# Pooled attention and gated MLP on one core: stages cut into one-engine parts with a written place for each, and other groupings in two transposes

## The chip, the cores and the metric

The kernel runs on one core of a Trainium2 chip. The metric is device time in microseconds (us) of one execution, less is better. The kernel before takes 604.04 us (median of three runs, 603.68 to 604.25).

## The reference, cut to what matters

Eight batches of 576 rows. Keys and values are averaged over groups of eight rows (72 pooled rows), eight heads of 64 columns attend to them, and the result (576 x 512) goes through a gated MLP whose spatial gate mixes the 576 rows.

```python
k_p = k.reshape(B, H, Sp, pool, D).mean(axis=3)          # Sp = 72, pool = 8
v_p = v.reshape(B, H, Sp, pool, D).mean(axis=3)
scores = scale * np.matmul(q, k_p.transpose(0, 1, 3, 2))
attn = np.exp(scores - max); attn = attn / (sum + 1e-09)
x = np.matmul(attn, v_p)                                 # heads side by side: (8, 576, 512)
h = np.maximum(x @ w_in, 0.0); u, v = h[..., :512], h[..., 512:]
v_n = (v - mean) / np.sqrt(var + 1e-06)
v_s = np.einsum('ts,bsd->btd', w_spatial, v_n) + b_spatial[None, :, None]
out = (u * v_s) @ w_out
```

`w_in` and `w_out` come in as 64-bit floats; all else is 32-bit.

## The kernel before

The 576 rows of a batch are five row tiles: four of 128 and a last one of 64 (tile 4). They are worked on in two halves, tiles 0 and 1 (256 rows) and tiles 2 to 4 (320 rows). The large products run in three passes over operands that are each split into a high and a low part (`_h`, `_l`).

A batch is a list of named stages, each a Python generator that yields between its parts:

- **K** loads the keys and sums each group of eight (on DVE), **KT** transposes the sums on TensorE into PSUM and copies them into the block-diagonal `kp_bd`. The 8 x 72 key rows stand one after the other in blocks of 128, so there are four full blocks and one of 64; the sum is written twice side by side (`kp`, 128 x 128 a block), so that a transpose yields it in both partition halves.
- **V**, **W**: the same sums for the values, then their split and masks (`vm_h`, `vm_l`, `vr`).
- **Q**c loads row tile c of the queries and transposes it; **S**c computes its scores and its softmax; **T**c transposes the probabilities P. A head pair has 144 score columns; the first 128 are transposed at once (`pm`), and the last 16 of all four pairs, the "rest of P" (`pr`, 64 columns), by themselves, in two transposes of 32 columns, into `rr`.
- S has two forms. In the plain one DVE subtracts the maximum, ACT takes one exponential over 576 columns and DVE sums. In the other (marked `~`) ACT takes eight exponentials of 72 columns with the maximum as bias and the sum as by-product.
- **A**hg multiplies P and the values for half h and head pair g into `xT`.
- **v**c, **u**hd: the two halves of x @ w_in (v by row tile with its normalisation, u transposed by half and block of 128 columns); **s**hd: the spatial product and the gate; **o**c: the product with w_out and the store. **o4** stores the last 64 rows of two batches at once.
- **wv**, **wu**, **wo**, **ws**, **wb**: loads and splits of the weights, once, spread over the first stretch of the program. A part of `w_in` can take its low part from three matmuls against identities (marked `^`) or from GpSimd (POOL).

Three strings (`FIRST`, `SECOND` for batch 0, `STEP` for all others, the last too) name the stages in an order. A name begins a stage or advances it by one part; `step()` after each v, u, s, o stage advances every stage that is under way by one part; and `needs()` lists what has to stand before a stage begins, so that a name may begin several others. One part often holds instructions of two or three engines. The recording keeps this order on TensorE (PE), DVE, ACT and POOL. The transfers, all on SyncE's queue (SP), are put in order by the framework. Each engine runs its own instructions strictly in its order and waits on semaphores for the others; PSUM has three buffers for the large products, three for transposes and A (`ps_t`), and one of two banks that KT and S share (`ps_s`).

Of the kernel before, what the change touches and what calls it, by code (L numbers as in the profile page):

```python
# [15 lines left out]
ORDERED = {getattr(mybir.EngineType, n) for n in ("PE", "DVE", "Activation", "Pool")}  # L16


# [9 lines left out]
FIRST = (  # L28
    "KT Q0 wv0~^ KT wv1^ Q0 wv0 wv1 S0~ wv0 Q1 wv1 wv0 S1~ S0 V T0 wv1 Q2 wv0 S1 wv2~^ S1 wv2 V wv2 "
    "wv1 wv2 wv2 W "  # L30
)
SECOND = (
# [6 lines left out]
)  # L39
STEP = (  # L40
    "Q1 . u00 u02 -T4 Q0 v1 -A13 -A10 -A12 S0 u01 -A11 v0 v4 S1 v2 Q4 Q2 v3 u03 u13 W T0 S2 u10 u12 "
    "u11 s00 s03 T1 s11 Q3 s01 +K s12 A00 s10 s02 A03 s13 S3 A02 . A01 . o0 S4 o2 T2 o1 +KT +V T3 o4 "
    "o3 "
# [8 lines left out]
def pooled_attention_gmlp(ctx: ExitStack, tc: tile.TileContext, q, k, v, w_in, w_sp, b_sp, w_out, out):  # L52
# [19 lines left out]
    RR = 2 * KR  # L72
    QK = 1.0 / (POOL * float(D) ** 0.5)
# [55 lines left out]
    def split(hi, lo, src):  # L129
        nc.scalar.activation(hi, src, AF.Copy)  # L130
        nc.vector.tensor_tensor(lo, src, f32(hi), op=ALU.subtract)  # L131

    def load_f64(hi, lo, src, alt, st=None):
# [10 lines left out]
        if len(src.shape) == 2:  # L144
            nc.sync.dma_start(out=st, in_=src.bitcast(U32).rearrange("p (n w) -> p n w", w=2))
        else:
            nc.sync.dma_start(out=st.rearrange("p (c n) w -> p c (n w)", c=NK), in_=src.bitcast(U32))
        low, high = st[:, :, 0], st[:, :, 1]
# [7 lines left out]
        nc.scalar.activation(x, high.bitcast(F32), AF.Abs, scale=2.0 ** -112)  # L156
        yield
# [4 lines left out]
        if "~" in alt:  # L162
            nc.vector.scalar_tensor_tensor(z, low, 2.0 ** -52, y, op0=ALU.mult, op1=ALU.mult)
        else:
            scaled = low.bitcast(F32)
            nc.scalar.activation(scaled, low, AF.Copy, scale=2.0 ** -52)
            nc.gpsimd.tensor_tensor(z, scaled, y, op=ALU.mult)
# [10 lines left out]
        else:  # L178
            nc.gpsimd.tensor_tensor(as_w(x), as_w(x), f32(hi), op=ALU.subtract)
            nc.gpsimd.tensor_tensor(lo, as_w(x), as_w(y), op=ALU.add)  # L180
# [28 lines left out]
    def load_w_sp(i):  # L209
# [3 lines left out]
        nc.sync.dma_start(out=st[:m], in_=w_sp[ts, :])  # L213
        a = ps_big()
# [6 lines left out]
        split(wT_h[:, :NC, ts], wT_l[:, :NC, ts], av)  # L221
        for r in range(2):
            nc.scalar.activation(wT_h[r * TL:(r + 1) * TL, NC, ts], t, AF.Copy)
        nc.vector.tensor_tensor(wT_l[:TL, NC, ts], t, f32(wT_h[:TL, NC, ts]), op=ALU.subtract)
# [27 lines left out]
    def att_keys(t, b, alt=""):  # L252

        rows = k[b].rearrange("h (s j) d -> (h s) (j d)", j=POOL)
        kp = pl.tile([P, NC + 1, 2, D], F32, name="kp", tag="kp")
        acc = ps_pool() if "^" in alt else None
        for r in range(2):
            st = pl.tile([P, 2, POOL * D], F32, name="st", tag="kv", bufs=3)
            nc.sync.dma_start(out=st, in_=rows[2 * r * P:2 * (r + 1) * P].rearrange("(n p) f -> p n f", p=P))
            n2 = slice(2 * r, 2 * r + 2)  # L260
            if acc is None:
                pool_sum(st, kp[:, n2])
            else:
                pool_pe(st, acc[:, n2, :])
            yield
        st = load_rest(rows[NC * P:])
        if acc is None:
            pool_sum(st, kp[:TL, NC:], nc.gpsimd if alt else nc.vector)
        else:
            pool_pe(st, acc[:TL, NC:, :])  # L270
            yield
            nc.scalar.copy(kp[:, :NC], acc[:, :NC, :].unsqueeze(2).broadcast_to([P, NC, 2, D]))
            nc.scalar.copy(kp[:TL, NC:], acc[:TL, NC:, :].unsqueeze(2).broadcast_to([TL, 1, 2, D]))
        t["k"] = kp

    def att_keys_t(kp, alt=""):

        kt = ps_s.tile([P, 2 * 512], F32, name="s_ps", tag="s")
        for n in range(NC + 1):
            m = P if n < NC else TL  # L280
            nc.tensor.transpose(out=kt[:, n * P:n * P + m], in_=kp[:m, n, :, :], identity=ident[:m, :m])
        yield
        keys = kt[:, :H * SP].rearrange("p (g e s) -> p g e s", g=NG, e=2)
        for e in range(2):
            es = slice(e * D, (e + 1) * D)
            copy = nc.vector.tensor_copy if alt else nc.scalar.copy
            copy(kp_bd[es, :, e * SP:(e + 1) * SP], keys[es, :, e, :])

    def att_values(t, b, alt=""):
# [6 lines left out]

        for r in range(2):
            g2 = slice(2 * r, 2 * r + 2)
            st = pl.tile([P, 2, POOL * D], F32, name="st", tag="kv", bufs=3)
            nc.sync.dma_start(out=st, in_=rows[g2, :P].rearrange("g p f -> p g f"))  # L300
            if acc is None:
                pool_sum(st, vp[:, g2, :], eng)
            else:
                pool_pe(st, acc[:, g2, :])
            yield
        st = load_rest(rows[:, P:])
        if acc is None:
            pool_sum(st, vq, eng)
        else:
            pool_pe(st, acc[:2 * RR, NG:, :])  # L310
            yield
            if "~" in alt:
                nc.scalar.copy(vp, acc[:, :NG, :])
                nc.scalar.copy(vq, acc[:2 * RR, NG:, :])
            else:
                vp, vq = acc[:, :NG, :], acc[:2 * RR, NG:, :]
# [7 lines left out]
    def att_values_split(vp, vr_s):  # L324
        for e in range(2):
            nc.scalar.activation(vm_h[:, :, e, :], vp, AF.Copy, scale=half_of[:, e:e + 1])
        yield
        for e in range(2):
            nc.vector.scalar_tensor_tensor(vm_l[:, :, e, :], vp, half_of[:, e:e + 1], f32(vm_h[:, :, e, :]),
                                           op0=ALU.mult, op1=ALU.subtract)  # L330
        nc.scalar.activation(vr[0:RR, :, 1, :], vr_s, AF.Copy)
        nc.scalar.activation(vr[2 * RR:, :, 1, :], vr_s, AF.Copy)
        nc.vector.tensor_tensor(vr[RR:2 * RR, :, 1, :], vr_s, f32(vr[0:RR, :, 1, :]), op=ALU.subtract)

    def att_q(t, b, c, alt=""):
# [3 lines left out]
        nc.sync.dma_start(out=qt[:m], in_=q[b, :, c * P:c * P + m, :].rearrange("h p d -> p h d"))  # L339
        qp = ps_tr()  # L340
# [8 lines left out]
    def att_softmax(t, c, alt=""):  # L349
# [12 lines left out]
        nc.vector.tensor_reduce(mx[:m], sv, axis=AX.X, op=ALU.max)  # L362
        e = pl.tile([P, H, SP], F32, name="e", tag="e", bufs=2)
# [9 lines left out]
        else:  # L373
# [3 lines left out]
            for h in range(H):  # L377
# [20 lines left out]
    def att_pt(t, c):  # L398
# [15 lines left out]
        trv = tr[:RR, :2 * m].rearrange("p (r t) -> p r t", r=2)  # L414
        for r in range(2):
            nc.tensor.transpose(out=trv[:, r, :], in_=pr[:m, 2 * r:2 * r + 2, :], identity=ident[:m, :m])
        yield
        split(mh[:, :, cs], ml[:, :, cs], tpv)
        for i in range(2):
            nc.scalar.activation(rr[i * RR:(i + 1) * RR, :, cs], trv, AF.Copy)  # L420
        nc.vector.tensor_tensor(rr[2 * RR:, :, cs], trv, f32(rr[:RR, :, cs]), op=ALU.subtract)
# [276 lines left out]
```

## Time and profile before

| | |
|---|---|
| median of three runs | 604.04 us |
| the profiled execution, its own time | 605.5 us |
| its span, first to last instruction | 603.7 us |
| mean granted TensorE clock | 0.992 |
| read from HBM, written | 36.08 MB, 9.44 MB |

The profile gives each engine's busy time. A matmul's record is longer than its share of the array's time, since the next one starts before it ends; what a matmul costs in a row of others is read from start to start. 32-bit matmuls that are no transposes stand as two records each. Line numbers are those of the kernel before, unless a row of the changed kernel is shown.

### The profile page before, as it was taken

How to read it: one execution, taken by the hardware profiler on the slowest of the kernel's cores; microseconds unless marked ns; L12 is line 12 of the kernel's file. 1: busy time of each engine (PE TensorE's matmuls, PEld its weight loads, DVE VectorE, ACT ScalarE, POOL GpSimd, SP SyncE). 2: the span in 40 equal slices, each digit the busy share in tenths (PEclk: the TensorE clock that was granted, in tenths of full speed). 3: DMA queues.
4: the chain of work that ended last, by engine and by line, in shares of the span. 5: the costliest groups of instructions: out<-in, count | busy, mean ns of one | idle time of the engine just before them, and what ended most of it. 6: DMA issues, size and time to landing. Idle time of an engine off the chain costs nothing.

```text
span 603.7 us, 9827 instructions
## 1 busy us (share of the span) xinstructions
PE 576.5 (95%) x3605; PEld 513.7 (85%) x3605; DVE 407.4 (67%) x854; ACT 296.8 (49%) x758; POOL 219.3 (36%) x280
## 2 busy tenths in 40 slices
PE   3776999999999999999999999999999999999997
PEld 3455989888997989888998889988998889988995
DVE  6799898968767486657866487766965488344520
ACT  3896576464634464254534355344533445343421
POOL 2237447913532064312442045321632135421440
PEclk9997999999999999999999999999999999999999
DMA  9933343271023210250121410242110300010002
GB/s 297 295 95 97 107 116 106 79 222 41 1 88 120 81 36 11 96 166 3 34 90 70 132 36 0 88 134 52 35 45 36 88 1 1 1 53 19 0 2 87
DMA packets 56688, 46.15 MB, mean 76 GB/s; under 512 B 39104, under 2 KB 41152, under 8 KB 56640
## 3 DMA queue, kind: packets, MB, share of 16 engines
q1 hardware_dynamic: 56640, 45.52, 25.4%
q8 instruction: 28, 0.46, 0.3%
q14 instruction: 20, 0.16, 0.1%
HBM read 36.08 MB, written 9.44 MB: 75 GB/s over the span
## 4 chain that ended last, share of the span: by engine, by line
PE 79%; ACT 12%; DVE 6%; issue 1%; DMA 1%; SPq 0%; POOL 0%; ACTq 0%; DVEq 0%
PE mm L557 17%; PE mm L536 16%; PE mm L477 15%; PE mm L517 9%; PE s_ps L355 5%; PE tp L343 3%; PE mm L492 2%; PE tp L412 2%; ACT e L379 2%; ACT ru L520 1%; PE mm L538 1%; PE mm L537 1%; PE tp L431 1%; PE tp L428 1%; PE tp L429 1%
## 5 line engine op out<-in xcount | busy, mean ns | idle before, releaser
L517 PE MATMUL mm<-xT,win_h 128*128 128x320 f32 (+1 forms) x512 | 105.2, 299 | 0.0
L387 POOL TENSOR_TENSOR pm<-e,rs 128x576 f32<-128x576 f32 (+1 forms) x40 | 49.5, 1238 | 117.2 <-DVE rs L384 52.6
L477 PE MATMUL mm<-win_h,xT 128*128 128x512 f32 x256 | 83.5, 407 | 0.0
L517 PEld LDWEIGHTS mm<-xT,win_h 128*128 128x128 f32 x512 | 82.6, 189 | 0.7
L557 PE MATMUL mm<-wout_h,gT 128*128 128x512 f32 x256 | 82.3, 402 | 0.0
L463 POOL TENSOR_TENSOR rstd<-rstd,neg_half 128x1 f32<-128x1 f32 (+1 forms) x40 | 23.5, 588 | 158.1 <-DVE rstd L462 158.1
L536 PE MATMUL mm<-wT_h,vn_h 128*128 128x320 f32 (+1 forms) x256 | 77.7, 303 | 0.8
L517 PE MATMUL mm<-xT,win_l 128*128 128x256 f32 (+1 forms) x256 | 75.7, 296 | 0.0
L536 PE MATMUL mm<-wT_h,vn_l 128*128 128x320 f32 (+1 forms) x256 | 75.5, 295 | 0.0
L536 PE MATMUL mm<-wT_l,vn_h 128*128 128x320 f32 (+1 forms) x256 | 75.4, 294 | 0.0
L548 POOL TENSOR_TENSOR gT<-g,gT 128x256 fp32r<-128x256 f32 x64 | 48.7, 766 | 61.3 <-ACT gT L547 61.3
L547 ACT ACTIVATE gT<-g 128x256 fp32r<-128x256 f32 x64 | 26.6, 417 | 79.3 <-DVE g L541 79.3
L131 DVE TENSOR_TENSOR pt_l<-tp,pt_h 128x512 fp32r<-128x512 f32 (+1 forms) x40 | 25.4, 635 | 49.0 <-ACT pt_h L130 48.7
L557 PEld LDWEIGHTS mm<-wout_h,gT 128*128 128x128 f32 x256 | 46.5, 189 | 11.2 <-issue 1.2
L477 PEld LDWEIGHTS mm<-win_h,xT 128*128 128x128 f32 x256 | 47.0, 191 | 9.4
L541 DVE TENSOR_TENSOR g<-mm,ru 128x320 f32<-128x320 f32 (+1 forms) x64 | 28.3, 448 | 38.5 <-PE mm L538 30.9
L561 ACT COPY ob<-mm 128x512 f32<-128x512 f32 x36 | 21.1, 587 | 64.4 <-PE mm L557 44.5
L355 PE MATMUL s_ps<-kp_bd,qT 128*128 128x144 f32 (+1 forms) x320 | 48.5, 296 | 4.3 <-ACT qT L346 2.2
L477 PE MATMUL mm<-win_l,xT 128*128 128x512 f32 x128 | 51.4, 401 | 0.0
L355 PEld LDWEIGHTS s_ps<-kp_bd,qT 128*128 128x128 f32 (+1 forms) x320 | 43.3, 186 | 9.4 <-ACT e L379 2.7
L557 PE MATMUL mm<-wout_l,gT 128*128 128x512 f32 x128 | 50.7, 396 | 0.0
L536 PEld LDWEIGHTS mm<-wT_h,vn_h 128*128 128x128 f32 x256 | 48.2, 188 | 2.2 <-ACT ru L520 2.0
(136 smaller groups left out, 1353.4 us busy)
## 6 DMA issues: line engine op xcount, KB each, us to landing
st<-in_k SPq DMA_DIRECT2D x16, 512.0 KB, 3.5
qt<-in_q SPq DMA_DIRECT2D x32, 256.0 KB, 2.9
st<-in_v SPq DMA_DIRECT2D x16, 512.0 KB, 3.6
out<-ob SPq DMA_DIRECT2D x32, 256.0 KB, 2.1
stw<-in_moe_w_in SPq DMA_DIRECT2D x8, 512.0 KB, 7.0
st<-in_moe_w_out SPq DMA_DIRECT2D x4, 512.0 KB, 3.4
st<-in_moe_w_spatial SPq DMA_DIRECT2D x4, 288.0 KB, 4.0
st_r<-in_k SPq DMA_DIRECT2D x8, 128.0 KB, 4.5
```

The lines of the kernel that those rows point to most:

```text
L131: nc.vector.tensor_tensor(lo, src, f32(hi), op=ALU.subtract)
L355: nc.tensor.matmul(s_ps[:m, g // 2, (g % 2) * 2 * SP:(g % 2 + 1) * 2 * SP], lhsT=qT[:, g, :m], rhs=kp_bd[:, g, :], start=True, stop=True,)
L387: nc.gpsimd.tensor_tensor(pm[:m], em, rs[:m].unsqueeze(2).broadcast_to([m, H, SP]), op=ALU.mult)
L463: nc.gpsimd.tensor_tensor(rstd[:m], rstd[:m], neg_half[:m], op=ALU.pow)
L477: nc.tensor.matmul(a, lhsT=xT[:, i, o + c * P:o + (c + 1) * P], rhs=w[:, i, DH:], start=(i == 0 and j == 0), stop=(i == NK - 1 and j == 2))
L517: nc.tensor.matmul(a, lhsT=w[:, i, d * P:(d + 1) * P], rhs=xT[:, i, o + ts.start:o + ts.stop], start=(i == 0 and j == 0), stop=(i == NK - ...
L536: nc.tensor.matmul(a, lhsT=x[:, c, ds], rhs=y[:, c, ts], start=(c == 0 and j == 0), stop=False)
L541: nc.vector.tensor_tensor(g, a, t["ru"][:, d, ts], op=ALU.mult)
L547: nc.scalar.activation(dst[:, d, 0, at:at + m], g[:, o:o + m], AF.Copy)
L548: nc.gpsimd.tensor_tensor(dst[:, d, 1, at:at + m], g[:, o:o + m], f32(dst[:, d, 0, at:at + m]), op=ALU.subtract)
L557: nc.tensor.matmul(a, lhsT=src[:, i, x, at:at + m], rhs=w[:, i, :], start=(i == 0 and j == 0), stop=(i == ND - 1 and j == 2))
L561: nc.scalar.copy(ob[:m], a)
```

## The change

It does five things.

1. Every stage is cut at each change of engine (more `yield`s), so that a part holds one engine's instructions. `run()` does nothing but advance the named stage by one part; `needs()`, `step()` and `begin()` are gone, and the strings name every part. SP is among the engines whose order is kept, so loads and stores have their place too. `SECOND` is gone: `FIRST` covers batch 0's attention and the weights up to batch 0's end, `STEP` is used for batches 1 to 6 and `LAST` for batch 7.
2. KT: two heads' first 64 pooled rows stand in one block (`kp`, four head pairs in two blocks of 128 x 128), the last eight rows of all eight heads in another (`kr`, 64 x 128). Three transposes take the place of five, in a `ps_t` buffer instead of `ps_s`. K loads in four transfers and a rest instead of two and a rest; the sums of `kp` are written once and not twice, and four copies instead of two fill `kp_bd`.
3. The rest of P: POOL writes `pr` twice side by side (two instructions), one transpose takes the place of two, and its rows come out twice, so that ACT copies 64 partitions at once for each pair of head pairs. DVE's subtraction is two instructions.
4. The forms chosen differ: the eight-exponential softmax is used for 18 of 40 tiles instead of 7; the value sums run on POOL for seven of eight batches (on DVE before), the rest of the keys on POOL for six of eight (one before); seven low parts of weights come from matmuls against identities instead of five.
5. What of the weights is loaded when: a part of `w_in` is loaded ahead of the keys.

```diff
-ORDERED = {getattr(mybir.EngineType, n) for n in ("PE", "DVE", "Activation", "Pool")}
+ORDERED = {getattr(mybir.EngineType, n) for n in ("PE", "DVE", "Activation", "Pool", "SP")}
 FIRST = (
-    "KT Q0 wv0~^ KT wv1^ Q0 wv0 wv1 S0~ wv0 Q1 wv1 wv0 S1~ S0 V T0 wv1 Q2 wv0 S1 wv2~^ S1 wv2 V wv2 "
...
+    "wv1~^ wv1 wv1 -K wv1 -K wv3~^ -K -Q0 -V -K -K wv1 -K -Q0 wv3 -Q0 wv3 wv2^ -KT wv1 -KT -Q1 -V -V -KT -S0~ "
...
 STEP = (
-    "Q1 . u00 u02 -T4 Q0 v1 -A13 -A10 -A12 S0 u01 -A11 v0 v4 S1 v2 Q4 Q2 v3 u03 u13 W T0 S2 u10 u12 "
...
+    "-s12 -A00 -s00 -A00 -S4 -A00 -s00 -s10 Q1 -s02 +K~ -T2 -s10 -s13 -s02 -s11 -s02 KT v1 -s03 -S4 -s03 KT "
...
 def att_keys_t(kp, kr, alt=""):
-        kt = ps_s.tile([P, 2 * 512], F32, name="s_ps", tag="s")
-        for n in range(NC + 1):
-            m = P if n < NC else TL
-            nc.tensor.transpose(out=kt[:, n * P:n * P + m], in_=kp[:m, n, :, :], identity=ident[:m, :m])
+        kt = ps_tr()
+        for r in range(2):
+            nc.tensor.transpose(out=kt[:, r * P:(r + 1) * P], in_=kp[:, r, :, :], identity=ident)
+        nc.tensor.transpose(out=kt[:, 2 * P:2 * P + 2 * RR], in_=kr[:, 0, :, :], identity=ident[:2 * RR, :2 * RR])
...
 def att_softmax(t, c, alt=""):
-        pr = pl.tile([P, NG, KR], F32, name="pr", tag="pr", bufs=2)
-        nc.gpsimd.tensor_tensor(pr[:m], em[:, 1::2, SP - KR:], rs[:m, 1::2].unsqueeze(2).broadcast_to([m, NG, KR]),
-                                op=ALU.mult)
+        pr = pl.tile([P, 2, 2, RR], F32, name="pr", tag="pr", bufs=2)
+        for i in range(2):
+            sh = [m, 2, 2, KR]
+            nc.gpsimd.tensor_tensor(
...
 def att_pt(t, c):
-        for r in range(2):
-            nc.tensor.transpose(out=trv[:, r, :], in_=pr[:m, 2 * r:2 * r + 2, :], identity=ident[:m, :m])
+        nc.tensor.transpose(out=tr[:, :m], in_=pr[:m], identity=ident[:m, :m])
...
     def run(b, order):
         for name in order.split():
...
-            again = [part for k, part in going if k == key]
-            if again:
-                advance(key, again[0])
-            else:
-                begin(key, **({"alt": name} if name[-1] in "~^" else {}))
-            if name[0] in ".vuso" and not again:
-                step()
+            make = (wl if key[0] < 0 else stages[key[0]] if key[0] < B else {}).get(key[1])
+            if make and key not in parts:
+                parts[key] = make(**({"alt": name} if name[-1] in "~^" else {}))
+            next(parts.get(key, iter(())), None)
```

Three places show how the order moves. First, the head of SP's queue: the transfers with which the program starts. Before:

```order
L259 DMA st<-in_k 128x2x512 x2
L249 DMA st_r<-in_k 64x512
L339 DMA qt<-in_q 128x8x64
L145 DMA stw<-in_moe_w_in 128x1024 x2
L339 DMA qt<-in_q 128x8x64
L300 DMA st<-in_v 128x2x512
```

And in the changed kernel:

```order
L165 DMA stw<-in_moe_w_in 128x1024
L289 DMA st<-in_k 128x1x512 x4
L165 DMA stw<-in_moe_w_in 128x1024
L276 DMA st_r<-in_k 64x1x512
L377 DMA qt<-in_q 128x8x64
L335 DMA st<-in_v 128x2x512
```

One part of `w_in` now stands ahead of all keys, and a second ahead of the rest of the keys and the first queries; batch 0's keys come in four transfers.

Second, PE in the middle of the program, at a KT and a T (`kp` the pooled keys, `pm` the probabilities, `pr` their rest). Before, the KT and the T that follows it between two o stages:

```order
L557 MATMUL mm<-wout_l,gT 128x512
L281 MATMUL s_ps<-ident,kp 128x128 x4
L281 MATMUL s_ps<-ident,kp 128x64
L412 MATMUL tp<-ident,pm 128x128 x4
L416 MATMUL tp<-ident,pr 32x128 x2
L557 MATMUL mm<-wout_h,gt 128x512 x2
```

In the changed kernel KT stands behind tile 4's scores and ahead of an A; this is the piece from there:

```order
L394 MATMUL s_ps<-kp_bd,qT 64x144 x4
L312 MATMUL tp<-ident,kp 128x128 x2
L313 MATMUL tp<-ident,kr 128x64
L477 MATMUL tp<-pt_h,vm_h 128x256
L478 MATMUL tp<-pt_h,vm_l 128x256
```

and a T of the same batch, 14 rows of an s stage later:

```order
L589 MATMUL mm<-wT_l,vb 128x320
L459 MATMUL tp<-ident,pm 128x128 x4
L461 MATMUL tp<-ident,pr 128x128
L587 MATMUL mm<-wT_h,vn_h 128x320
L587 MATMUL mm<-wT_h,vn_l 128x320
```

KT is three transposes instead of five, T five instead of six, and both stand among other stages than before.

Third, POOL in the middle of the program, up to the probabilities that T0 transposes (`rstd` a v stage's reciprocal deviation, `vn_l` its low part, `gT` and `gt` a gate's low part, `st`, `st_r` the loaded values, `vp`, `vq` their sums). Before:

```order
L387 TENSOR_TENSOR pm<-e,rs 64x576
L389 TENSOR_TENSOR pr<-e,rs 64x64
L463 TENSOR_TENSOR rstd<-rstd,neg_half 128x1 x2
L486 TENSOR_TENSOR vn_l<-vv,vn_h 128x512
L387 TENSOR_TENSOR pm<-e,rs 128x576
L389 TENSOR_TENSOR pr<-e,rs 128x64
```

In the changed kernel, the second half of the value sums onward:

```order
L257 TENSOR_TENSOR st<-st 128x2x256
L257 TENSOR_TENSOR st<-st 128x2x128
L262 TENSOR_TENSOR vp<-st 128x128
L513 TENSOR_TENSOR rstd<-rstd,neg_half 128x1
L257 TENSOR_TENSOR st_r<-st_r 64x256
L257 TENSOR_TENSOR st_r<-st_r 64x128
L262 TENSOR_TENSOR vq<-st_r 64x64
L513 TENSOR_TENSOR rstd<-rstd,neg_half 128x1
L601 TENSOR_TENSOR gT<-g,gT 128x256
L601 TENSOR_TENSOR gt<-g,gt 128x64
L513 TENSOR_TENSOR rstd<-rstd,neg_half 128x1
L428 TENSOR_TENSOR pm<-e,rs 128x576
```

The value sums, which were DVE's, now stand in POOL's queue ahead of the first probabilities of the next batch, and a gate's low part between them. On PE there stand, between the v stage whose `rstd` is the last one here (v2) and T0: v4, v3 and Q3. On DVE the row sum of S0 stands directly behind v2's statistics.

More of the change, by code (lines that the diff above doesn't have):

```diff
@@ L286, in att_keys_t @@
             copy = nc.vector.tensor_copy if alt else nc.scalar.copy
-            copy(kp_bd[es, :, e * SP:(e + 1) * SP], keys[es, :, e, :])
+            copy(kp_bd[es, :, e * SP:e * SP + KM], main[es])
+            copy(kp_bd[es, :, e * SP + KM:(e + 1) * SP], rest[es, :, e, :])
+            if e == 0:
+                yield
     def att_values(t, b, alt=""):
@@ L295, in att_values @@
         acc = ps_pool() if "^" in alt else None
+        sts, g2 = [], [slice(2 * r, 2 * r + 2) for r in range(2)]
         for r in range(2):
[L298 to L302, printed above, removed]
-            else:
-                pool_pe(st, acc[:, g2, :])
+            sts.append(pl.tile([P, 2, POOL * D], F32, name="st", tag="kv", bufs=3))
+            nc.sync.dma_start(out=sts[r], in_=rows[g2[r], :P].rearrange("g p f -> p g f"))
             yield
         st = load_rest(rows[:, P:])
+        yield
+        for r in range(2):
+            if acc is None:
+                pool_sum(sts[r], vp[:, g2[r], :], eng)
+            else:
+                pool_pe(sts[r], acc[:, g2[r], :])
+            yield
         if acc is None:
@@ L327, in att_values_split @@
         yield
+        for r in range(2):
+            nc.scalar.activation(vr[2 * r * RR:(2 * r + 1) * RR, :, 1, :], vr_s, AF.Copy)
+        yield
         for e in range(2):
@@ L561, in moe_o @@
         nc.scalar.copy(ob[:m], a)
+        yield
         if c < NC:
@@ L630, in advance @@
-    def advance(key, part):
-        if next(part, True):
-            going.remove((key, part))
-            done.add(key)
-    def step():
-        for key, part in list(going):
-            advance(key, part)
-    def begin(key, **alt):
-        make = (wl if key[0] < 0 else stages[key[0]] if key[0] < B else {}).get(key[1])
-        if key in begun or not make:
-            return
-        whole, first = ([], []) if key[0] < 0 else needs(*key)
-        for other in whole:
-            begin(other)
-            while other not in done:
-                advance(other, next(part for k, part in going if k == other))
-        for other in first:
-            begin(other)
-        begun.add(key)
-        part = make(**alt)
-        next(part)
-        going.append((key, part))
+    parts = {}
@@ L676 @@
+    run(B - 1, LAST)
 _INS = ["q", "k", "v", "moe_w_in", "moe_w_spatial", "moe_b_spatial", "moe_w_out"]
```

138 lines of the change are left out of this document (63 added, 75 removed), and 35 rows, old and new, of tables (FIRST, LAST, SECOND, STEP).

## The prediction

> **What bounds the kernel now.** I read the page's busy times and slices first. The rows are the engines' busy time and count, and PE's busy tenths in 40 slices.
>
> ```profile
> PE 576.5 (95%) x3605; PEld 513.7 (85%) x3605; DVE 407.4 (67%) x854; ACT 296.8 (49%) x758; POOL 219.3 (36%) x280
> PE   3776999999999999999999999999999999999997
> ```
>
> TensorE is the bound from the fifth slice to the last; the four first slices are not full. Busy times by stretch put numbers on that (columns: stretch, length, then PE, PEld, DVE, ACT, POOL busy with counts, granted clock, DMA share, GB/s).
>
> ```profile
> 0.00:49.40 49.40, 28.26 (x131) 19.61 (x132) 37.61 (x90) 36.66 (x120) 15.92 (x24) 0.96 0.73 218
> 54.30:60.00 5.70, 5.70 (x24) 4.64 (x23) 5.43 (x11) 2.30 (x7) 3.24 (x4) 0.70 0.44 121
> 60.00:599.00 539.00, 537.91 (x3432) 485.98 (x3431) 359.58 (x750) 253.68 (x624) 195.67 (x249) 1.00 0.21 63
> ```
>
> From 60 us on PE idles for 539.00 - 537.91 = 1.1 us in all. So two things can make this kernel faster: an earlier start of the dense part, and less work on PE in it. A better order of the other engines has almost nothing left to win there, and something to lose. The start is read in the timeline:
>
> ```profile
> 4.01 1.15 DVE L230 TENSOR_TENSOR st<-st 128x512 f32<-128x512 f32 x2 [3.16 <-DMA st<-in_k]
> 9.25 0.66 ACT L156 ACTIVATE x<-stw 128x512 f32<-128x512 f32 x1 [7.24 <-DMA stw<-in_moe_w_in]
> 49.11 1.11 PE L412 MATMUL tp<-ident,pm 128*128 128x128 f32 x4 [5.10 <-POOL pm L387]
> 49.18 0.20 DVE L384 RECIPROCAL rs<-sm 64x8 f32<-64x8 f32 x1
> 49.30 2.21 DVE L230 TENSOR_TENSOR st<-st 128x512 f32<-128x512 f32 x2
> 52.84 0.68 DVE L131 TENSOR_TENSOR pt_l<-tp,pt_h 128x512 fp32r<-128x512 f32 x1
> 53.67 0.43 PE L412 MATMUL tp<-ident,pm 64*128 64x64 f32 x4 [1.31 <-DVE pt_l L131]
> 54.31 0.72 PE L477 MATMUL mm<-win_h,xT 128*128 128x512 f32 x2
> ```
>
> The first v stage (L477), the marker of the dense part, starts at 54.31 us, right behind T4. DVE is the engine that sets it: 37.61 us of work up to S4's reciprocal (49.38 us), with 49.38 - 4.01 - 37.6 = 7.8 us of waits since its first key sum. Then 4.9 us pass until the first v, with batch 1's key sum (49.30, to 52.9) ahead of the `pt_l` that T4 waited for.
>
> **The change, part by part.** *Start.* Counted in the order, DVE has nearly the same work ahead of S4's reciprocal: seven weight parts, five maxima, both pooled sums, four `xT`; one `z`, one plain softmax more, one T's `pt_l` and `rr` and one `wT_l` fewer, narrower `kp`. By the rows of before that is 38 us, within 0.5 us of the old count. The weight part that is now first on SP should land where the first keys did, at 4.0 us, instead of 9.25; behind ACT's 0.66 us DVE starts at 4.7. Without waits S4's reciprocal ends at 4.7 + 38 = 42.7 us, with all 7.8 us of them at 50.5. Behind it two `pt_l` and an `rr` (2 x 0.68 + 0.5) stand before T4, and no key sum any more: 2.9 us to the first v with T4's own 0.6 and the hops, or 4.9 as before. So the first v starts between 45.5 and 55.4 us. I take half the waits, since DVE gets work of two kinds (weights, keys) from the first microsecond on, and S1's eight exponentials (2.45 us on ACT) become one: 42.7 + 3.9 + 2.9 = 49.5 us. **Term: -4.8 us**, ends -8.8 and +1.1.
>
> *Transposes.* Rows of PE's timeline around a KT and a T:
>
> ```profile
> 328.47 0.80 PE L281 MATMUL s_ps<-ident,kp 128*128 128x128 f32 x5
> 329.20 0.66 PE L412 MATMUL tp<-ident,pm 128*128 128x128 f32 x4
> ...
> 302.58 0.60 PE L412 MATMUL tp<-ident,pm 128*128 128x128 f32 x4
> 303.01 0.38 PE L416 MATMUL tp<-ident,pr 128*32 128x128 f32 x2
> 303.15 0.39 PE L536 MATMUL mm<-wT_h,vn_h 128*128 128x320 f32 x1
> 303.38 0.31 PE L536 MATMUL mm<-wT_h,vn_l 128*128 128x320 f32 x1
> 303.52 0.31 PE L536 MATMUL mm<-wT_l,vn_h 128*128 128x320 f32 x1
> ```
>
> Start to start four transposes take 0.43 us, 0.109 each. The two of `pr` take 0.14, but the matmul behind them keeps the next waiting 0.23 instead of 0.14: the last transpose's share is paid there. So one `pr` transpose less is worth 0.109 us, or 0.03 if that delay stays as it is. KT loses two of its four full transposes (0.22 us of 0.73); the one of 64 rows stays. In batches 1 to 7: 7 x 0.22 + 28 x 0.109 + 7 x 0.06 (tile 4, half the width) = **-5.0 us**; the other end is -2.6. The first batch's fall into the start. More PSUM copies (four into `kp_bd`, two DVE subtractions a T) lie beside PE's work; ACT and DVE have the room (49% and 67% busy).
>
> In the Trainium skill, "TensorE: Matmul & The Clock Gate", Part 4, a transpose of 128 x 128 costs about 275 ns in a kernel. The trace agrees only with that as one record's length; the spacing is 0.109 us, and here the trace is used. By the page the 49 transposes would be worth 13.5 us as an estimate, and the forecast 588 us; the spacing leaves that no chance of its own.
>
> *Weights.* Two more low parts come from three matmuls against identities, later than the first v. One such set, start to start:
>
> ```profile
> 20.65 1.02 PE L173 MATMUL mm<-x,ident 128*128 128x512 f32 x2
> 21.98 0.60 PE L343 MATMUL tp<-ident,qt 128*128 128x128 f32 x4
> ```
>
> 1.33 us each: **+2.7 us**, or nothing if both fall into idle time.
>
> *Moves to ACT and POOL.* Eleven more tiles take the softmax of eight exponentials, and seven batches sum their values on POOL:
>
> ```profile
> 15.71 2.45 ACT e L379 x16
> 57.86 1.77 POOL L230 TENSOR_TENSOR st_r<-st_r 64x256 f32<-64x256 f32 x2
> 59.71 0.52 POOL L235 TENSOR_TENSOR kp<-st_r 64x128 f32<-64x128 f32 x1
> L179 POOL TENSOR_TENSOR x<-x,wout_h 128x512 f32<-128x512 f32 x4 | 5.9, 1475 | 1.3 <-ACT wout_h L169 1.3
> L548 POOL TENSOR_TENSOR gT<-g,gT 128x256 fp32r<-128x256 f32 x64 | 48.7, 766 | 61.3 <-ACT gT L547 61.3
> ```
>
> ACT gains 11 x (2.45 - 0.7) = 19 us and ends near 315; POOL gains per batch two halves of 1.48 + 0.77 + about 0.5, a rest of about 2.3 us, and second `pr` instructions, and ends near 285; DVE falls to near 360. All stay far below PE, so the sums cost nothing by themselves; what counts is what is queued behind them. On POOL that is `pm` of S0, for which T0 waits. The last input of that chain is v2, whose statistics stand on DVE ahead of S0's sum. Handoffs of before, in the start and at 300 us:
>
> ```profile
> 58.99 0.60 ACT L480 ACTIVATE vv<-mm 128x512 f32<-128x512 f32 x1 [2.38 <-PE mm L477]
> 60.77 0.15 DVE L462 TENSOR_SCALAR rstd<-mv 128x1 f32<-128x1 f32 x1
> 300.46 0.75 DVE L372 TENSOR_REDUCE sm<-e 128x8 f32<-128x576 f32 x1 [0.83 <-ACT e L370]
> 301.83 1.16 POOL L387 TENSOR_TENSOR pm<-e,rs 128x576 f32<-128x576 f32 x1 [5.68 <-DVE rs L384]
> ```
>
> From v2's last matmul: 60.92 - 58.99 = 1.93 us to `rstd`, then 302.99 - 300.46 = 2.53 from the sum to the end of `pm`, 4.46 us. PE has v4, v3 and Q3 in that time; a v takes 2.82 us:
>
> ```profile
> 54.38 4.51 PE mm L477 x12
> 60.05 2.82 PE mm L477 x12
> ```
>
> 2.82 + 8/12 x 2.82 + 0.36 = 5.06 us, so 0.6 us are spare. **Term: 0**, ends -1.1 (all idle time goes) and +14 (below).
>
> *SP's order, and the last batch.* SP's DMAs keep their place behind each other; K's two more issues a batch (0.5 us each, by the first rows of the queue) meet a queue that mostly waits. LAST can win nothing, since PE is full up to the last matmul; its tail, one copy and one store, stays. Both 0, give or take 1 us.
>
> The sum is -4.8 - 5.0 + 2.7 = -7.1 us. The profiled execution took 605.5 us (603.7 and 1.8 around it), 1.5 over the median; differences carry over: 604.04 - 7.1 = **596.9 us**.
>
> **Rivals.** *The start does not get earlier.* DVE waits as before, for scores held up by the one PSUM buffer of S (each S waits for the exponentials before it). For it: nothing in the change adds such a buffer. Against it: weights land earlier and KT leaves that buffer. Then only PE's work counts: 604.04 - 2.3 = 601.7 us. Chance 0.17.
>
> *Everything fits.* No DVE waits at the start (-8.8), none on PE later (-1.1), and the first v at full clock: it took 4.51 instead of 2.82 us, in the stretch with clock 0.70 behind the 5.1 us wait (-1.7). 604.04 - 8.8 - 2.3 - 1.1 - 1.7 = 590.1 us. Chance 0.13.
>
> *POOL becomes what PE waits for.* Slower than before. DVE's two key sums of 1.15 us (row at 4.01, POOL idle) took 2.21 at 49.30, with POOL at work: the two hold each other up. Eight more POOL instructions a batch stand among DVE's sums; if each loses 0.4 us, `pm` of S0 comes 3 us later, T0 waits beyond its 0.6 us, and with it all PE work: 7 x 2.4 = +17 - 7.1, or 614 us. It decides from a wait of 1.0 us a batch on. Against it: about 19 us of PE work stand between T4 and T0, and POOL has 11 to do there. Chance 0.11.
>
> The Trainium skill, "SBUF — State Buffer", section "Who interferes with whom", has a rule for this: a DVE instruction with two SBUF inputs and a POOL instruction that reads SBUF exclude each other for a whole instruction. The pair 1.15 and 2.21 agrees. By that rule each of POOL's sums could wait up to 0.73 us; price and chance above go by the row alone.
>
> **How the numbers follow.** The forecast has 0.59 and covers 593.5 to 600.5 us. The range reaches to the second rival and past the first, 590.0 to 604.5 us; outside it lie most of the slow rival and a little below. A measurement of this kernel tells about 0.2% (1.2 us) from no change. Faster: 0.59 + 0.13 + two thirds of 0.17 = 0.83; the same 0.06; slower 0.11.
>
> **What would show it.** The first v should start at 49.5 us; between T's `pm` and the next stage one transpose; PE idle from there to the end under 2 us; no wait of T for `pm` behind the start; DVE near 360, ACT 315, POOL 285 us busy. The forecast is wrong if T0 waits in every batch, if PE idles again between 50 and 90 us because weights come late, or if the first v starts behind 53 us.

## The result, and the profile after

The changed kernel takes **617.29 us** (median of 4 runs, 616.82 to 617.54) where the kernel before takes 604.14 (4 runs, 603.68 to 604.26): a ratio of **1.0218, 95% interval 1.0200 to 1.0236**, 2.2% slower. The forecast was 596.9 us, with a range of 590.0 to 604.5.

The page has PE's work shorter and its span longer (busy times, and busy tenths in 40 slices):

```profile
span 615.7 us, 9982 instructions
PE 573.3 (93%) x3557; PEld 513.8 (83%) x3557; DVE 346.1 (56%) x809; ACT 301.5 (49%) x937; POOL 266.6 (43%) x394
PE   1177889999999999999999999999999999999997
```

The span is 12.0 us longer than before (603.7). The loss has to be in the first slices. Busy times of stretches show it, two of the start, then from the first v stage (L527, now at 67.95 us) to 90, and from there to the last matmul (columns as before: length, PE, PEld, DVE, ACT, POOL, clock, DMA share, GB/s):

```profile
0.00:15.00 15.00, 2.05 (x2) 0.50 (x2) 2.30 (x5) 2.57 (x3) 2.72 (x10) 1.00 0.20 70
15.00:30.00 15.00, 2.07 (x6) 1.38 (x7) 4.78 (x17) 0.66 (x1) 0.00 (x0) 1.00 0.63 189
67.95:90.00 22.05, 18.98 (x110) 16.66 (x110) 14.79 (x32) 10.84 (x28) 10.62 (x12) 0.92 0.39 118
90.00:612.00 522.00, 522.00 (x3307) 473.70 (x3305) 292.13 (x683) 255.06 (x800) 237.53 (x353) 1.00 0.21 63
```

From 90 us on PE never waits: whatever POOL, DVE and ACT were given, it hides there. In the first 30 us PE is busy for 4.1 us, and in the first 15 the transfers hardly run: 70 GB/s at a share of 0.20 where the kernel before moved 295 at 0.93:

```profile
0.00:15.00 15.00, 5.81 (x22) 4.52 (x23) 9.27 (x24) 5.59 (x9) 3.67 (x11) 1.00 0.93 295
```

The timeline of the changed kernel names what came late:

```profile
4.47 0.66 ACT L177 ACTIVATE x<-stw 128x512 f32<-128x512 f32 x1 [2.46 <-DMA stw<-in_moe_w_in]
15.80 0.69 DVE L257 TENSOR_TENSOR st<-st 128x512 f32<-128x512 f32 x1 [8.30 <-DMA st<-in_k]
26.54 0.69 DVE L257 TENSOR_TENSOR st<-st 128x512 f32<-128x512 f32 x1 [8.75 <-DMA st<-in_k]
27.66 0.66 ACT L177 ACTIVATE x<-stw 128x512 f32<-128x512 f32 x1 [20.68 <-DMA stw<-in_moe_w_in]
29.12 1.11 PE L382 MATMUL tp<-ident,qt 128*128 128x128 f32 x4 [11.02 <-DMA qt<-in_q]
32.20 1.09 PE L394 MATMUL s_ps<-kp_bd,qT 128*128 128x144 f32 x3 [1.24 <-ACT kp_bd L321]
67.95 0.50 PE L527 MATMUL mm<-win_h,xT 128*128 128x512 f32 x1
```

The first weight part comes about when it was forecast: ACT starts on it at 4.47 us, and it was to land at 4.0. The first two key sums start at 15.80 and 26.54 us; before it was 4.01 and 5.67. The second weight part and the first q come behind them, and the first scores at 32.20 instead of 11.95. Two of these rows in the kernel before:

```profile
5.67 1.15 DVE L230 TENSOR_TENSOR st<-st 128x512 f32<-128x512 f32 x2
11.95 1.33 PE L355 MATMUL s_ps<-kp_bd,qT 128*128 128x144 f32 x4 [2.24 <-ACT qT L346]
```

The chain of waits of this start (start, length, what; SPq is SP's queue in the act of issuing) and the transfers in 40 slices of 0.7 us from 0 to 28 us (busy tenths of the 16 DMA engines, and GB/s):

```profile
1.18 0.73 SPq L289
1.96 0.54 SPq L289
2.54 4.81 SPq L289
7.40 5.00 SPq L289
12.45 4.98 SPq L165
17.46 11.04 DMA st_r<-in_k
```
```profile
DMA  0028920111111111111111111379797336961698
GB/s 0 0 82 281 304 91 3 41 50 53 50 53 50 53 50 50 53 53 50 50 53 53 50 50 53 88 231 336 246 287 180 103 64 187 398 196 56 217 293 252
```

The four key transfers of batch 0 (L289, 256 KB each) are issued behind the first weight part. From about 5 to 17 us one tenth of the 16 engines is busy and 50 to 53 GB/s flow. The first two issues take 0.73 and 0.54 us, the next ones about 5 us each, which is 256 KB at 53 GB/s (4.9 us): the queue takes a new transfer only as fast as an old one drains. So the issue of w_in (L165) behind them begins at 12.45 us (in experiment 1 below at 3.83), and the last 64 key rows (`st_r`), ready to go at 17.46, land 11.04 us later.

The form of the transfers is one candidate for the cause. Each reads `keys[r, e, :, :KM, :]`: two heads, of each 64 of its 72 pooled rows of 2048 bytes. The 64 rows don't join up with the next head's, so the outermost dimension of the source is 2. The kernel before read 128 rows on end. The rival theory is the order on SP: weights ahead of keys, and four issues in place of two.

### The profile page after: what moved, and what is told of

Its sections match the earlier page's. It is cut to its first block, busy times and chain, and to the rows that moved or that the text cites. A ratio compares the mean times of both kernels' runs of the same rounds, so it can differ in the third digit from the quotient of the medians.

```text
span 615.7 us, 9982 instructions
## 1 busy us (share of the span) xinstructions
PE 573.3 (93%) x3557; PEld 513.8 (83%) x3557; DVE 346.1 (56%) x809; ACT 301.5 (49%) x937; POOL 266.6 (43%) x394
## 4 chain that ended last, share of the span: by engine, by line
PE 88%; DMA 4%; SPq 3%; ACT 2%; DVE 2%; issue 0%; DVEq 0%; ACTq 0%
PE mm L568 17%; PE mm L587 17%; PE mm L610 16%; PE mm L527 14%; PE s_ps L394 6%; PE tp L459 3%; PE mm L542 2%; PE tp L382 2%; DMA st<-in_k 2%; SPq L289 2%; DMA st_r<-in_k 2%; PE tp L477 1%; PE mm L589 1%; PE mm L588 1%; PE tp L480 1%; PE tp L478 1%
## 5 line engine op out<-in xcount | busy, mean ns | idle before, releaser
L428 POOL TENSOR_TENSOR pm<-e,rs 128x576 f32<-128x576 f32 (+1 forms) x40 | 47.0, 1174 | 93.1 <-DVE rs L425 87.5
L568 PEld LDWEIGHTS mm<-xT,win_h 128*128 128x128 f32 x512 | 83.9, 190 | 1.8
L527 PE MATMUL mm<-win_h,xT 128*128 128x512 f32 x256 | 82.0, 401 | 0.0
L587 PE MATMUL mm<-wT_h,vn_h 128*128 128x256 f32 (+1 forms) x256 | 76.3, 298 | 0.0
L587 PE MATMUL mm<-wT_h,vn_l 128*128 128x256 f32 (+1 forms) x256 | 75.6, 295 | 0.0
L587 PE MATMUL mm<-wT_l,vn_h 128*128 128x256 f32 (+1 forms) x256 | 75.4, 295 | 0.0
L536 POOL TENSOR_TENSOR vn_l<-vv,vn_h 128x512 fp32r<-128x512 f32 x32 | 41.7, 1320 | 52.5 <-ACT vn_h L534 52.5
L527 PEld LDWEIGHTS mm<-win_h,xT 128*128 128x128 f32 x256 | 46.7, 188 | 10.0
L394 PE MATMUL s_ps<-kp_bd,qT 128*128 128x144 f32 (+1 forms) x320 | 49.7, 301 | 4.2 <-ACT e L420 2.8
L149 ACT ACTIVATE xT<-tp 128x256 fp32r<-128x256 f32 (+1 forms) x64 | 25.0, 414 | 58.1 <-PE tp L480 57.8
L527 PE MATMUL mm<-win_l,xT 128*128 128x512 f32 x128 | 50.7, 396 | 0.0
L568 PEld LDWEIGHTS mm<-xT,win_l 128*128 128x128 f32 x256 | 48.7, 190 | 0.0
L587 PEld LDWEIGHTS mm<-wT_h,vn_l 128*128 128x128 f32 x256 | 48.2, 188 | 0.0
```

The lines of the kernel that those rows point to most:

```text
L394: nc.tensor.matmul(s_ps[:m, g // 2, (g % 2) * 2 * SP:(g % 2 + 1) * 2 * SP], lhsT=qT[:, g, :m], rhs=kp_bd[:, g, :], start=True, stop=True,)
L428: nc.gpsimd.tensor_tensor(pm[:m], em, rs[:m].unsqueeze(2).broadcast_to([m, H, SP]), op=ALU.mult)
L527: nc.tensor.matmul(a, lhsT=xT[:, i, o + c * P:o + (c + 1) * P], rhs=w[:, i, DH:], start=(i == 0 and j == 0), stop=(i == NK - 1 and j == 2))
L536: nc.gpsimd.tensor_tensor(t["vn_l"][:, c, :], vv, f32(t["vn_h"][:, c, :]), op=ALU.subtract)
L568: nc.tensor.matmul(a, lhsT=w[:, i, d * P:(d + 1) * P], rhs=xT[:, i, o + ts.start:o + ts.stop], start=(i == 0 and j == 0), stop=(i == NK - ...
L587: nc.tensor.matmul(a, lhsT=x[:, c, ds], rhs=y[:, c, ts], start=(c == 0 and j == 0), stop=False)
```

## The experiments

Each ratio is against the kernel before on the same chip. The start of one and the same order differs by up to 2 us between executions, so small differences are read from first v to first v in the trace.

**1. The rows outermost.** The changed kernel, with another order of the rows over the partitions:

```diff
-keys = k[b].rearrange("(r a e) (s j) d -> r e a s (j d)", r=2, e=2, j=POOL)
+keys = k[b].rearrange("(r a e) (s j) d -> r e s a (j d)", r=2, e=2, j=POOL)
-nc.sync.dma_start(out=sts[r][:, e, :], in_=keys[r, e, :, :KM, :])
+nc.sync.dma_start(out=sts[r][:, e, :], in_=keys[r, e, :KM, :, :])
-main = kt[:, :2 * P].rearrange("p (g s) -> p g s", g=NG)
+main = kt[:, :2 * P].rearrange("p (r s a) -> p r a s", r=2, a=2)
-copy(kp_bd[es, :, e * SP:e * SP + KM], main[es])
+copy(kp_bd[es, :, e * SP:e * SP + KM].rearrange("p (r a) s -> p r a s", a=2), main[es])
```

> The changed kernel, with the pooled rows of a key half in the order (row, head) instead of (head, row) over the partitions: each of the four key transfers has its 64 rows outermost instead of its 2 heads; the copies into kp_bd undo the order. Same bytes, same four issues, same place on SP. Theory 'form' (a transfer with 2 outermost runs on few of the 16 DMA engines, which is why the first 15 us moved 70 GB/s at a share of 0.20, and holds back what is issued behind it): second key sum before 8 us instead of 26.5, DMA share of 0:15 over 0.8, first v at 49 to 53 instead of 68.0, and 596 to 600 us. Theory 'order' (weights ahead of the keys on SP and four issues a batch in place of two make the start late): 614 to 618 us, nothing lands earlier.

Measured: **595.57 us** (594.7 to 598.1), ratio 0.9828 (0.9801 to 0.9855). Its windows, key sums, first scores and first v:

```profile
0.00:15.00 15.00, 5.15 (x14) 2.61 (x15) 9.08 (x25) 5.96 (x12) 2.72 (x10) 0.96 0.88 285
49.73:75.00 25.27, 23.52 (x133) 20.18 (x133) 17.89 (x39) 12.61 (x33) 15.60 (x19) 0.93 0.40 116
75.00:592.00 517.00, 516.99 (x3283) 469.72 (x3282) 288.76 (x674) 253.25 (x796) 233.99 (x346) 1.00 0.21 63
```
```profile
7.90 0.68 DVE L257 TENSOR_TENSOR st<-st 128x512 f32<-128x512 f32 x1
9.80 1.14 DVE L257 TENSOR_TENSOR st<-st 128x512 f32<-128x512 f32 x2
14.16 1.08 PE L394 MATMUL s_ps<-kp_bd,qT 128*128 128x144 f32 x3 [1.55 <-ACT kp_bd L321]
49.73 0.72 PE L527 MATMUL mm<-win_h,xT 128*128 128x512 f32 x2
```

The second key sum starts at 9.80, a little later than expected but not held by a transfer any more (no wait stands behind the row). The same bytes in as many issues at the same place: the order is out, and the form is worth the whole loss.

**2. One head a transfer.** The same rows, in the changed kernel's own order:

```diff
-nc.sync.dma_start(out=sts[r][:, e, :], in_=keys[r, e, :, :KM, :])
+for a in range(2):
+    nc.sync.dma_start(out=sts[r][a * KM:(a + 1) * KM, e, :], in_=keys[r, e, a, :KM, :])
```

> The changed kernel, with each of its key transfers cut in two by head: eight of 64 rows each (64 x 512 floats, 128 KB) instead of four of 2 x 64; nothing else differs. 'Form': the outermost dimension is 64 here too, so the start is that of the run with rows over heads, within 1.5 us (four more issues of 0.5 us on SP at the start): 596 to 601 us. 'Order', where the number of issues is what costs: slower than the changed kernel, 617 to 625 us.

Measured: 596.56 us (596.31 to 598.75), ratio 0.9857 (0.9831 to 0.9883), first v at 49.65 us. Twice the issues, and the loss is gone as well.

**3. The slow transfers alone, in the kernel before.**

```diff
-nc.sync.dma_start(out=st, in_=rows[2 * r * P:2 * (r + 1) * P].rearrange("(n p) f -> p n f", p=P))
+if b == 0:
+    keys = k[b].rearrange("(r a e) (s j) d -> r e a s (j d)", r=2, e=2, j=POOL)
+    for e in range(2):
+        nc.sync.dma_start(out=st[:, e, :], in_=keys[r, e, :, :64, :])
+else:
+    ...
```

> The kernel before, in which batch 0 alone loads its two halves of keys by the four transfers of the changed kernel (64 of 72 pooled rows of each head, so batch 0's keys are other rows than the reference's), at the same place on SP, ahead of everything. 'Form': 512 KB of keys at the rate of the changed kernel, the first sum at about 14 us instead of 4.0 and the second at about 25 instead of 5.7, w_in and q behind them; PE's first scores at 28 to 32 instead of 12, and 616 to 624 us. 'Order': two more issues of 0.5 us, 604 to 606 us.

Measured: 623.66 us (623.17 to 624.58), ratio 1.0298 (1.0276 to 1.0321), 18 us lost by four transfers of one batch. DVE's first key sums, and a stretch in which nothing but keys is under way:

```profile
13.70 1.15 DVE L230 TENSOR_TENSOR st<-st 128x512 f32<-128x512 f32 x2 [12.85 <-DMA st<-in_k]
24.24 1.15 DVE L230 TENSOR_TENSOR st<-st 128x512 f32<-128x512 f32 x2 [8.93 <-DMA st<-in_k]
3.50:13.50 10.00, 0.00 (x0) 0.00 (x0) 0.00 (x0) 0.00 (x0) 0.00 (x0) 1.00 0.13 51
```

The profile gives the mean share of the 16 engines and not each one's; two of 16 at work would be 0.125.

**4. The keys behind weights and q on SP.** Of the changed kernel's start only SP's order changes:

```diff
-"wv1~^ wv1 wv1 -K wv1 -K wv3~^ -K -Q0 -V -K ...
+"wv1~^ wv3~^ -Q0 wv1 wv1 -K wv1 -K -K -V -K ...
```

> The changed kernel with its four key transfers as they are, but on SP behind the second part of w_in and the first q in batch 0 (the third key transfer, of 64 rows, stays behind them as well). 'Form': the keys still take some 24 us, so the scores of batch 0 start near 32 us as in the changed kernel, while the second weight part lands near 6 instead of 27.7: 608 to 616 us. 'Order': what the keys held up comes early, most of the loss is gone, 597 to 604 us.

Measured: 617.18 us (616.64 to 618.16), ratio 1.0191 (1.0169 to 1.0214), 1.2 us past what 'form' expected (the kernel before takes 605.61 us on this chip, 1.5 more than in the result). The second weight part was worked on from 7.27 us instead of 27.66, and no gain clear of the noise came of it (1.0218 for the changed kernel, and the first v at 67.3 us against 67.95): the keys' second half is what the start needs.

```profile
28.06 1.15 DVE L257 TENSOR_TENSOR st<-st 128x512 f32<-128x512 f32 x2 [9.40 <-DMA st<-in_k]
31.98 1.33 PE L394 MATMUL s_ps<-kp_bd,qT 128*128 128x144 f32 x4 [1.06 <-ACT kp_bd L321]
```

**5 to 7. How many outermost runs.** The kernel before, batch 0's keys in four transfers as in the third experiment, but each of 4, 8 or 16 heads with 32, 16 or 8 rows; here for 4 (`heads` counts over all batches):

```diff
+heads = k.rearrange("b h (s j) d -> (b h) s (j d)", j=POOL)
+for e in range(2):
+    nc.sync.dma_start(out=st[:, e, :], in_=heads[4 * r:4 * (r + 1), e * (P // 4):(e + 1) * (P // 4), :])
```

> As the run of the kernel before with slow keys, but each of batch 0's four key transfers takes 4 heads of 32 pooled rows, instead of 2 heads of 64: same 256 KB, same rows of 2048 bytes, same partitions (batch 0's keys are other rows than the reference's). 'Form', with as many DMA engines at work as there are outermost runs: two engines gave about 53 GB/s, so four give 106, the first 512 KB lands at 2 + 5 us (first key sum near 8 us instead of 13.7), the second near 13 instead of 24.2, DMA share 0.25 while only keys run. If only the two-headed form is slow for another reason (two heads' rows in one place of the memory, say), the sums start near 4 and 6 us.

> The same with 8 heads of 16 rows: 'form' gives 212 GB/s and a share of 0.5 while only keys run, the first key sum near 5 us, the second near 7.5.

> The same with 16 heads of 8 rows (two batches' heads): 'form' gives a share near 0.9, the first key sum at about 4 us and the second near 6, as in the kernel before, and a time within 3 us of it.

The first key sum of each run, and a stretch in which no engine has work yet, in the order 4, 8, 16; the last line is a stretch of the kernel before:

```profile
9.75 1.15 DVE L230 TENSOR_TENSOR st<-st 128x512 f32<-128x512 f32 x2 [8.89 <-DMA st<-in_k]
3.50:7.00 3.50, 0.00 (x0) 0.00 (x0) 0.00 (x0) 0.00 (x0) 0.00 (x0) 1.00 0.29 104
6.51 1.15 DVE L230 TENSOR_TENSOR st<-st 128x512 f32<-128x512 f32 x2 [5.66 <-DMA st<-in_k]
3.50:6.00 2.50, 0.00 (x0) 0.00 (x0) 0.00 (x0) 0.00 (x0) 0.00 (x0) 1.00 0.49 172
5.39 1.15 DVE L230 TENSOR_TENSOR st<-st 128x512 f32<-128x512 f32 x2 [4.54 <-DMA st<-in_k]
3.50:5.00 1.50, 0.00 (x0) 0.00 (x0) 0.00 (x0) 0.00 (x0) 0.00 (x0) 1.00 1.01 246
3.00:4.00 1.00, 0.00 (x0) 0.00 (x0) 0.00 (x0) 0.00 (x0) 0.35 (x1) 1.00 1.03 389
```

| Outermost runs | Share of the 16 engines | GB/s | First and second key sum, us | Time, against before |
|---|---|---|---|---|
| 2 (run 3) | 0.13 | 51 | 13.70, 24.24 | +18.1 us |
| 4 | 0.29 | 104 | 9.75, 15.60 | +9.2 us |
| 8 | 0.49 | 172 | 6.51, 10.67 | +6.1 us |
| 16 | 1.01 | 246 | 5.39, 7.88 | +4.6 us |
| before: 128 rows | 1.03 | 389 | 4.01, 5.67 | 0 |

The three rows in the middle are single executions. The share follows the number of outermost runs, as 2, 4, 8 and 16 engines of 16 would (1.01 and 1.03 are a full share). In all stretches but the first, transfers behind the keys have been issued as well (in the run with 16 from 3.39 us on), so these figures are not the keys' alone. The sums came 1.5 to 3.2 us later than expected for 4 and 8. The first v came 8.9, 4.1 and 3.1 us later than before. With 16 runs there was still a loss of 4.6 us (expected: within 3), with first scores 2.9 us later than before; whether that is the four issues, the eight-row runs or in part the scatter of a single execution stays open.

**8. The transpose of `pr`, twice.** On top of experiment 1:

```diff
-nc.tensor.transpose(out=tr[:, :m], in_=pr[:m], identity=ident[:m, :m])
+for n in range(2):
+    nc.tensor.transpose(out=tr[:, n * P:n * P + m], in_=pr[:m], identity=ident[:m, :m])
```

> The run with rows over heads, with the transpose of pr in every T issued twice, the second into columns that nothing reads: the cost of the transpose that the change takes away, doubled. By the spacing of transposes that the prediction used (0.109 us, 0.06 in tile 4) a batch takes 0.50 us longer: a pair of batches 138.0 us instead of 137.02 (69.91 + 67.11 from first v to first v), and the time is 4 us more, about 599.5. If the delay of the matmul behind it stays the same (the prediction's other end), 0.15 us a batch, 1 us in all. If a transpose costs its record's length, 0.4 us, 1.7 us a batch, 14 us in all.

Measured: ratio 0.9904 (0.9871 to 0.9938), against 0.9828 without it. First v stages two batches apart, in the kernel before, in experiment 1 and here:

```profile
268.84 0.48 PE L477 MATMUL mm<-win_h,xT 128*128 128x512 f32 x1
407.99 0.48 PE L477 MATMUL mm<-win_h,xT 128*128 128x512 f32 x1
250.45 0.39 PE L527 MATMUL mm<-win_h,xT 128*128 128x512 f32 x1
387.47 0.39 PE L527 MATMUL mm<-win_h,xT 128*128 128x512 f32 x1
247.92 0.39 PE L528 MATMUL mm<-win_h,xT 128*128 128x512 f32 x1
385.94 0.39 PE L528 MATMUL mm<-win_h,xT 128*128 128x512 f32 x1
```

The pairs take 139.15, 137.02 and 138.02 us: the extra transposes cost 0.50 us a batch, to the hundredth what their spacing says. The changed kernel's own pair (269.89 to 406.91) is 137.02 as well, slow transfers and all.

**9. The sums of v on DVE.** On top of experiment 1, every `V~` in the orders written as `V`.

> The run with rows over heads, with the sums of v of every batch on DVE instead of POOL, at the same places in DVE's order. The prediction put the move of these sums to POOL at 0: then a pair of batches stays at 137.0 us and the time within 1 us of 595.6. The rival 'POOL becomes what PE waits for', if it is there in part, gives a shorter pair here, by 1 us or more; if DVE has become short of room instead, a longer one.

Measured: 609.22 us (607.35 to 610.2), ratio 1.0061 (1.0044 to 1.0079), slower even than before. A pair takes 138.8 us, and single batches lose more. PE's waits between 100 and 500 us, of which experiment 1 has none:

```profile
PE tp L479 <- DVE pt_l L151: 3.1, 1, 3.1
PE mm L527 <- DVE xT L151: 3.1, 5, 0.6
```

So the move to POOL is no cost, and in this order PE needs it: with the sums in DVE's row, what PE reads (`pt_l`, `xT`) comes late.

**10. One weight part fewer by matmuls.** On top of experiment 1, `wo3~^` written as `wo3~`.

> The run with rows over heads, with the low part of wo3 made by two POOL subtractions and additions instead of three matmuls against identities: one of the two weight parts that the change adds to PE. The prediction: 1.33 us of PE each, behind the first v: the time from first v to the last matmul goes from 542.9 to 541.6 us. If the set falls into idle time of PE: no change, within 0.3 us; if POOL's later low part is waited for: longer.

Measured: 603.06 us (601.38 to 605.87), ratio 0.9962 (0.9939 to 0.9984). From first v to last matmul it took 547.6 instead of 542.9 us: 4.7 longer, where 1.3 shorter was expected. (Experiment 1's profiled execution is the slowest of its four, with a granted clock of 0.93 from 49.7 to 75 us. Experiments 2 and 12, at 1.00 there, take 541.5 and 541.3.) PE's wait and DVE's:

```profile
PE tp L477 <- DVE xT L151: 5.4, 1, 5.4
DVE y L184 <- POOL wout_l L204: 5.0, 1, 5.0
```

POOL now finishes `wout_l` late, and with it gives back the buffer of `y` late (two buffers, shared with the output rows); DVE waits 5.0 us for the buffer in the middle of its row, and PE 5.4 us for the `xT` behind it. From 110 to 120 us the granted clock is 0.61 and 0.70 in the two halves, and 1.00 in experiment 1, so more than the wait is lost. The set of matmuls that was left out takes 1.32 us in experiment 1 (110.32 to 111.64), as priced, but it spared POOL the work that is late here.

**11. No order of its own for the last batch.** On top of experiment 1:

```diff
-    run(B - 1, LAST)
+    run(B - 1, STEP)
+    run(B, STEP)
```

> The run with rows over heads, with the last batch in the order of the other batches (STEP twice, the second time with nothing of a next batch in it) instead of LAST. The prediction: an order of its own for the last batch wins 0, give or take 1 us, since PE was full up to its last matmul in the kernel before. If this holds for an order as such, the time stays within 2 us of 595.6. Rival: STEP's gaps are filled by the stages of a next batch, which the last one has not; PE then waits for softmax and statistics in the last 60 us, 10 to 25 us longer, and LAST only keeps what the planner of before did by itself.

Measured: 603.02 us (601.86 to 605.93), ratio 0.9974 (0.9953 to 0.9995). From batch 6's first v to the last matmul it took 143.5 instead of 138.0 us, 5.5 longer. PE's waits there come to 3.3 us, and the one long wait is for the low part of the gate (the other 2 us of the 5.5 stay open):

```profile
PE mm L610 <- POOL gT L601: 2.6, 1, 2.6
```

Between the two expectations: LAST has nothing to win over the kernel before, where PE was idle for 1.1 us in all from 60 us on, but STEP without a next batch leaves gaps.

**12. Two key transfers a batch.** Experiment 1, with both heads e in one transfer:

```diff
-for e in range(2):
-    nc.sync.dma_start(out=sts[r][:, e, :], in_=keys[r, e, :KM, :, :])
+nc.sync.dma_start(out=sts[r], in_=keys[r, :KM])
```

where `keys` is now `r s a e (j d)`.

> The run with rows over heads, with the two transfers of a key half made one ([64 rows][2 heads a][2 heads e], 512 KB): two issues a batch fewer on SP, as many as in the kernel before, the 64 rows outermost. It prices the number of issues by itself, which the prediction put at 0, give or take 1 us. If an issue counts at the start (0.65 us each there), w_in's second part, q and the first scores come 1.3 us earlier than in the run with rows over heads (first scores at 12.9 instead of 14.2) and the time is 594 to 595; if not, the first v stays at 47.8 to 49.8 and the time within 1 us of 595.6. The two-batch period stays 137.02 in both cases.

Measured: 595.89 us (594.55 to 599.36), ratio 0.9855 (0.9829 to 0.9881); first scores at 14.97, first v at 49.19. No difference: two more issues, with 64 rows outermost, cost nothing.

The versions of experiments 1, 2 and 12 beat both kernels and cannot be told from each other: 1.4 to 1.7% under the kernel before, and 3.5 to 3.8% under the changed one.

## Why the prediction was wrong, step by step

**The step that failed** is that of SP's order: "K's two more issues a batch (0.5 us each, by the first rows of the queue) meet a queue that mostly waits", put at 0, give or take 1 us. It counted issues and bytes, and not the form of the transfers. The issues do cost nothing (experiments 2 and 12). But a transfer with two outermost runs moves 51 to 53 GB/s, at the share of two DMA engines, and near the head of the queue it holds the start. The term was +19 to +22 us: span 615.7 of the changed kernel against 596.3, 594.8 and 594.2 in experiments 1, 2 and 12, in which the form is mended. Against experiment 1, 18.2 of the 19.4 lie ahead of the first v (67.95 against 49.73), and 1.2 behind it, where DVE waits 1.0 us for the second key half of batch 1 too: PE's idle time from the first v on is 3.1 us here (22.05 - 18.98) and 1.8 there (25.27 - 23.52). The third experiment has about the same price from the other side, +18 us in the kernel before.

The Trainium skill, "DMA: Bandwidth & Descriptors", section "Why a DMA increments its semaphore by 16 and not by 1", has the rule that speaks of this: a transfer runs on the largest number of engines up to 16 that divides the outermost dimension (not 1) of both its sides. The runs with 2, 4, 8 and 16 outermost runs agree, at shares of 0.13, 0.29, 0.49 and 1.01, and so do those with 64 (0.88 over the first 15 us of experiment 1).

**The start** (-4.8 us, first v at 49.5) was right for a kernel in which the keys arrive: 49.73 with rows over heads, and 47.8 to 49.7 in all the runs on that base. The way there was right too: in experiment 1 S4's reciprocal ends at 46.2 us (forecast 46.6), and 3.5 us lie between it and the first v (forecast 2.9). Its premise that DVE has two kinds of work "from the first microsecond on" hung on the failed step.

**Transposes** (-5.0): 0.109 and 0.06 us apiece were right for `pr` (experiment 8), and not the other end of 0.03; the transposes of KT were not varied. The 275 ns of the Trainium skill ("TensorE: Matmul & The Clock Gate", Part 4) agrees with the length of a record, 278 ns on average for `pr` in experiment 1, and not with what one transpose more costs. A batch became 1.07 us shorter, against 0.72 by this term; where the rest lies stays open.

**Two more weight parts** (+2.7): the price of a set stands, but leaving one out does not give it back (experiment 10). From first v to last matmul experiment 1 needs 2.8 us less than before (542.9 against 545.7), and experiments 2 and 12 need 4.2 and 4.4 less; the two terms together said 2.3 less, so they were somewhat too small.

**Moves to ACT and POOL** (0): right; all stay below their forecast loads (DVE 346.1 us, ACT 301.5, POOL 266.6), and PE waits for none of them from 90 us on. **The last batch** (0): right against the kernel before.

**The rivals.** The slower one, POOL at 614 us, comes close to the measured time by chance and is wrong all the same: there is no wait for `pm` in the dense part. Right sign, wrong cause. The first one had the start no earlier, but for scores that wait for exponentials: PE waits for these 2.8 us in all (1.8 before), and 11.0 us once for a q behind the keys. The other terms, -7.1 us in sum, come near what is left with the form mended: experiment 1 is 10.0 us under the kernel before on its chip (595.57 against 605.61; the interval of its ratio spans 8.8 to 12.1), and the spans of the profiled executions differ by 7.4 to 9.5 (experiments 1 and 12).

**From batch 2 on the slow transfers cost nothing**: the pair takes 137.02 us with them and without. A batch's keys need some 20 us of two engines (1 MB at 53 GB/s), beside 68 us of PE work, and PE has no wait from 90 us on.

## What to carry to other kernels

Of a transfer that a change rewrites, read the shape as well as the bytes and the issues: the outermost dimension of its source set the share of the DMA engines that it got (here for 2, 4, 8 and 16), and a slice that keeps rows from joining across heads can take it from 128 to 2. Such a transfer is harmless where the queue runs ahead, and delays the end where it stands first; so price the start apart from the steady state. A move that looks like a cost on the busiest engine may be what keeps a buffer or another engine's row clear, so undo it alone before calling it a loss.

## What the runs showed of the hardware that was not expected

- Transfers on two engines hold up the issuing of what comes next: the third and fourth key transfer and the w_in behind them each held SP's queue about 5 us (4.81, 5.00, 4.98), the time in which one earlier transfer drains.
- What is issued behind them lands late too, though its outermost dimension is larger (8 heads, 128 rows): the 64 last key rows, issued at 17.46 us, landed 11.04 us later; on the second weight part, whose issue began at 12.45, ACT could start at 27.66. That these transfers wait for their share on the two busy engines is inferred, not shown.
- If the number of engines is read from the share, one engine moved about 25 GB/s of 2048-byte rows (51 on two, 104 on four, 172 on eight). All 16 came to nearly 16 times that: 389 GB/s from 3 to 4 us in the kernel before, with 128 rows outermost. With 16 runs of eight rows it was 246 at the same full share, in a stretch in which q and w_in have been issued too; what of that the form costs stays open.
